# Sparse attention and gated products in float32 on one core: the order of all steps but TensorE's listed anew, sums divided between VectorE and GpSimd

## The chip, the cores and the metric

One core of a Trainium2 chip. The time is device microseconds of one execution; the number given is the median of a kernel's runs.

## The reference

```python
def _attn_ref(q, k, v):                 # (8, 8, 576, 64) each
    scores = scale * np.matmul(q, k.transpose(0, 1, 3, 2))
    rel = pos[:, None] - pos[None, :]
    mask_local = (rel >= 0) & (rel < 32)                                 # heads 0 to 3
    mask_strided = (rel >= 0) & (pos[None, :] % 32 == pos[:, None] % 32)  # heads 4 to 7
    ...
    attn = np.exp(scores - max); attn /= sum
    return np.matmul(attn, v)

def _moe_ref(x, w_gate, w_val, w_out):  # x (4608, 512), w_gate and w_val (512, 1536), w_out (1536, 512)
    gate = 1.0 / (1.0 + np.exp(-(x @ w_gate)))
    return gate * (x @ w_val) @ w_out
```

The attention's output, its heads side by side, is the `x` of the second function.

## The kernel before

All products run in float32 accuracy on TensorE: each operand is split into a high part and a low remainder, and three products (high x high, low x high, high x low) are added in PSUM. ScalarE rounds off the high part (`x`, `hx`, `xh`, `ph` steps), VectorE subtracts it from the whole for the low part (`y`, `hy`, `xl`, `pw` steps: lines 651, 998, 916, 856).

The 4608 tokens are nine blocks of 512. Attention of a batch is four pieces (two local, two strided, two heads each), numbered n = 0 to 23 from batch 2 on. Of a piece, `S` are the scores (TensorE), `M`, `A`, `U` masking, maximum and its subtraction (VectorE), `E` the exponential (ScalarE), `N`, `W` the sum and its division (VectorE), `B` four turns of the matrix by pairs of VectorE's transposes (line 515), `X` the product with the values (TensorE), `H` and `R` copies of it (ScalarE).

Blocks 0, 1 and 2 are computed plainly, with twelve slices f: `g`, `v` the gate and value products of 2.7 us, `s` the sigmoid out of the gate's only bank, `m` gate times value, `x`, `y` the split, `o` or two `oh` the output products. Blocks 3 to 8 go in pairs, k = 3, 5, 7, with seven products of half matrices in place of eight. For that the weights are first kept in device memory in seven sets: `pl` and `po` copy four of them plainly (SP's queue), and of the other sets `pa` adds the words of a weight (line 842), `pb` makes four sums or differences of them (line 847), `ph`, `pw` split and `pd` stores them (lines 864, 865). `r` loads a group of sets back into a ring of buffers. For each pair of blocks `xd` makes four differences of the inputs for each half c (line 904), which `xh`, `xl` split. Then come for six pairs of slices q: `G` and `V`, the half products p (line 930), `c` and `ad` which take them out of PSUM (lines 952, 957), `sg` and `mu` sigmoid and gate (lines 965, 974), and `ta`, `tb`, `tc`, `td`, sums of the five products kept as `hid` (line 980). Then the output stage: `Oa`, `Ob` are groups of three products (line 1009) for p = 1, 2, 6, 5, 7, 3, 4 and q = 0 to 5, 84 groups or 252 products, and `hx`, `hy` split the operand of each q and p into rooms for five of them (`hh`, `hl` and `ops`). `ok` copies a sum out of PSUM (line 1021), `oa` adds to it (line 1025), `os` stores it. In the output stage of k = 3 and 5 the `xd`, `xh`, `xl` steps of the next pair are made.

The order of everything is written by hand: ORDER (line 82) is a list of 2870 step names with their numbers, and each step issues its instructions when its name comes; each engine, and each queue, works through its own in that order:

```python
    for n, (what, kind) in enumerate(zip(names, kinds)):
        STEPS[kind](*(int(i) for i in what[len(kind) :].split(".") if i))
```

Which engine a step runs on is fixed in STEPS (line 1038) and in its function; before, `pa`, `pb`, the four `t` sums and three of four `xd` are GpSimd's, and the second `xd` and all `pw`, `xl`, `hy` VectorE's. Rooms are single: `sum` tiles share `t`, `h2` and `h0` with the `xd` tiles and some `ot` tiles, so a step waits until the last reader of the tile before has done.

## Time and profile before

| | |
|---|---|
| median of 3 runs | 936.42 us (933.55 to 936.65) |
| the profiled execution, its own time | 935.28 us |
| its span, first to last instruction | 933.50 us |
| TensorE busy | 904.4 us, 97% |
| VectorE busy | 675.0 us, 72% |
| ScalarE busy | 476.4 us, 51% |
| GpSimd busy | 334.1 us, 36% |

A row of a timeline has start and duration in us from the start of the span, the engine (PE TensorE's products, PEld its weight loads, DVE VectorE, ACT ScalarE, POOL GpSimd, SP the DMA queue), the line of the code, the operation, and output <- inputs by name. A row of a group has the number of instructions behind `x`, then busy us, mean ns of one, and the idle time of the engine before them with what ended it. Products are pipelined: the next starts before the one before has ended, and the row of one product has a longer time than the step from start to start.

### The profile page before, as it was taken

The page shows a single profiled execution, that of the slowest core. Times are in us where ns is not written, and L with a number is a line of the kernel's source. Part 1 is how long each engine was busy: PE and PEld are TensorE (multiplying, and loading weights), DVE is VectorE, ACT ScalarE, POOL GpSimd, SP SyncE. Part 2 cuts the span into 40 slices and gives each one's busy share as a digit, 9 for nine tenths or more (in the row PEclk, how much of TensorE's full clock was granted, in tenths as well). Part 3 has the DMA queues.
Part 4 walks back from the last instruction along what each step waited for, and adds up shares of the span by engine and source line. Part 5 has one row for each costly group of instructions (what it writes and reads, how often), then busy time and mean ns, then how long its engine had stood idle before and what let it go on. Part 6 is the DMA issues. An engine that isn't in the chain of part 4 may idle for free.

```text
span 933.5 us, 18880 instructions
## 1 busy us (share of the span) xinstructions
PE 904.4 (97%) x7498; PEld 732.8 (79%) x7498; DVE 675.0 (72%) x1028; ACT 476.4 (51%) x854; POOL 334.1 (36%) x387
## 2 busy tenths in 40 slices
...
GB/s 350 355 204 96 192 140 162 162 196 170 304 351 185 112 168 203 285 294 289 248 281 195 173 213 243 217 232 182 198 180 147 190 272 166 218 180 208 196 208 132
DMA packets 116871, 198.26 MB, mean 212 GB/s; under 512 B 7600, under 2 KB 58800, under 8 KB 116784
## 3 DMA queue, kind: packets, MB, share of 16 engines
...
q8 instruction: 59, 0.97, 0.4%
...
## 4 chain that ended last, share of the span: by engine, by line
PE 73%; DVE 14%; DMA 4%; POOL 4%; issue 3%; ACT 2%; SPq 0%; DVEq 0%; POOLq 0%; ACTq 0%
PE p L930 16%; PE oc L1009 14%; PE d L930 13%; PE o L658 8%; PE v L627 8%; PE g L627 8%; DVE pt L515 3%; POOL sum L847 2%; DVE xs L916 2%; DVE hl L998 2%; DMA sets<-sum 2%; PE x L548 1%; DVE ops L998 1%; POOL sum L842 1%; PE s L406 1%
## 5 line engine op out<-in xcount | busy, mean ns | idle before, releaser
L930 PE MATMUL p<-xs,ring 128*128 128x512 f32 x864 | 208.6, 393 | 2.6 <-ACT hid L952 2.1
L930 PEld LDWEIGHTS p<-xs,ring 128*128 128x128 f32 x864 | 162.3, 189 | 38.1 <-ACT hid L952 3.1
L930 PE MATMUL d<-xs,ring 128*128 128x512 f32 x648 | 156.2, 390 | 0.2 <-DVE e L957 0.2
L980 POOL TENSOR_TENSOR hid<-hid,hid 128x512 f32<-128x512 f32 x45 | 64.7, 1438 | 250.8 <-DVE hid L974 250.1
L930 PEld LDWEIGHTS d<-xs,ring 128*128 128x128 f32 x648 | 121.3, 188 | 26.0 <-DVE e L957 0.7
L515 DVE STREAM_TRANSPOSE pt<-sb 32x320 f32<-32x320 f32 (+1 forms) x224 | 120.0, 536 | 4.1
L1009 PE MATMUL oc<-hh,ring 128*128 128x512 f32 x312 | 109.0, 394 | 0.0
L957 DVE TENSOR_TENSOR e<-e,d 128x512 f32<-128x512 f32 x54 | 36.9, 684 | 78.6 <-ACT e L952 40.1
L658 PE MATMUL o<-w,hh 128*128 128x512 f32 x288 | 90.7, 396 | 0.0
L842 POOL TENSOR_TENSOR sum<-w 128x256 f32<-128x256 f32 x68 | 55.5, 837 | 97.8 <-DMA sets<-sum 57.9
L627 PE MATMUL g<-xh,w 128*128 128x512 f32 x256 | 86.0, 393 | 3.2 <-ACT e L635 2.0
L998 DVE TENSOR_TENSOR hl<-hid,hh 128x512 fp32r<-128x512 f32 x78 | 66.4, 861 | 28.8 <-ACT hh L994 28.7
L627 PE MATMUL v<-xh,w 128*128 128x512 f32 x256 | 85.4, 390 | 0.4 <-DVE e L640 0.4
L847 POOL TENSOR_TENSOR sum<-sum 128x128 f32<-128x128 f32 x144 | 81.3, 567 | 10.0
L1009 PE MATMUL oc<-ops,ring 128*128 128x512 f32 x288 | 79.0, 394 | 2.7 <-DVE ops L998 2.4
L1009 PE MATMUL oc<-hl,ring 128*128 128x512 f32 x156 | 62.0, 398 | 9.3 <-DVE hl L998 9.3
L994 ACT CAST hh<-hid 128x512 fp32r<-128x512 f32 x78 | 48.4, 621 | 41.7 <-PE oc L1009 24.6
L1009 PEld LDWEIGHTS oc<-hh,ring 128*128 128x128 f32 x312 | 59.2, 190 | 12.8 <-ACT hh L994 0.4
L1009 PEld LDWEIGHTS oc<-ops,ring 128*128 128x128 f32 x288 | 53.5, 189 | 17.6 <-DVE ops L998 6.9
L952 ACT COPY e<-p 128x512 f32<-128x512 f32 x54 | 31.5, 584 | 69.6 <-PE p L930 66.0
L965 ACT ACTIVATE e<-e 128x512 f32<-128x512 f32 x54 | 34.1, 632 | 62.8 <-DVE e L957 62.7
L658 PEld LDWEIGHTS o<-w,hh 128*128 128x128 f32 x288 | 52.8, 188 | 11.4
...
## 6 DMA issues: line engine op xcount, KB each, us to landing
ring<-sets SPq DMA_DIRECT2D x126, 512.0 KB, 4.3
...
```

The lines of the kernel that those rows point to most:

```text
L515: nc.vector.transpose(dst[to : to + LB, :, col : col + LB], src[part * LB : (part + 1) * LB, :, h * LB : (h + 1) * LB])
L627: nc.tensor.matmul(o, w, x, start=first and n == 0, stop=last and n == len(todo) - 1)
L658: nc.tensor.matmul(acc[k][i], h[:, i * P : (i + 1) * P], w, start=f == 0 and n == 0, stop=f == NF - 1 and n == 2,)
L842: nc.gpsimd.tensor_tensor(to, part(wh[f][i], c), part(wl[f][i], c), op=ALU.add)
L847: nc.gpsimd.tensor_tensor(u[:, to], u[:, x], u[:, y], op=op)
L930: nc.tensor.matmul(to, w[:, (wi * 2 + c) * P : (wi * 2 + c + 1) * P], x[xi][:, c], start=p in (1, 2, 5) and c == j == 0, stop=c == 1 and j ...
L957: nc.vector.tensor_tensor(x, x, two[m, 1], op=ALU.add)
L965: nc.scalar.activation(x, x, AF.Sigmoid)
L980: by.tensor_tensor(h[to], h[x], h[y], op=ALU.subtract)
L994: nc.scalar.copy(ops[q, p][0], hidden_tile(k, q, KEPT[str(p)]))
L998: by.tensor_tensor(hl, hidden_tile(k, q, KEPT[str(p)]), hh.bitcast(F32), op=ALU.subtract)
L1009: nc.tensor.matmul(chains[m, at], w[:, (wi * 2 + m) * P : (wi * 2 + m + 1) * P], x[xi], start=p in (1, 2, 5) and q == j == 0, stop=q == PA ...
```

## The change

The list ORDER from block 1's first product on is another one: the steps of TensorE stand in it in the same order as before, those of all other engines and the DMA steps at other places. Seven kinds of steps can now be given to either of VectorE and GpSimd, by a letter behind the kind (`v` for VectorE, `p` for GpSimd), and the list says which: `pav` 10 of 36, `pbv` 4 of 36, `tav` 4, `tbv` 5, `tcv` 6, `tdv` 4 of 18 each, `xdv` 12 of 24; `pwp` 2 of 36, `xlp` 3 of 42, `hyp` 4 of 126. Of the 24 `xd`, 6 were VectorE's before.

```diff
@@ -101,117 +101,117 @@
-o0.10 fH1.3 LV0 y0.11 wu11.2 fL1.3 pa0.0.0 fR1.3 wl11.2 pa0.0.1 g1.0 pl0 pb0.0.0 v1.0 s1.0 pb0.0.1 oh0.11.0 m1.0 x1.0 S0.0 e0.0 y1.0 d0.0 oh0.11.1 LQ1
+o0.10 fH1.3 LV0 y0.11 wu11.2 fL1.3 pa0.0.0 fR1.3 wl11.2 pa0.0.1 pl0 g1.0 pb0.0.0 v1.0 s1.0 pl2 pb0.0.1 oh0.11.0 m1.0 e0.0 x1.0 S0.0 e0.1 y1.0 oh0.11.1
...
@@ -834,26 +834,26 @@
             nc.sync.dma_start(to[:, 0, n], a[:, 0])
             nc.sync.dma_start(to[:, 1:3, n], b)
 
-    def sum_words(q, i, c):
+    def sum_words(q, i, c, by=nc.gpsimd):
         n = (q * 2 + i) * 2 + c
         u = sums[q, i, c] = work.tile([P, 4, P], F32, tag=("t" if i < 2 else "h2", "h0")[n % 2], name=f"sum{q}_{i}_{c}")
         for at, f in ((0, 2 * q), (1, 2 * q + 1)):
             to = u[:, at::2] if i == 2 else u[:, 2 * at : 2 * at + 2]
-            nc.gpsimd.tensor_tensor(to, part(wh[f][i], c), part(wl[f][i], c), op=ALU.add)
-
-    def sum_parts(*n):
+            by.tensor_tensor(to, part(wh[f][i], c), part(wl[f][i], c), op=ALU.add)
+
+    def sum_parts(*n, by=nc.gpsimd):
         u = sums[n]
         for to, x, y, op in ((3, 2, 3, ALU.add), (2, 0, 2, ALU.subtract), (0, 3, 0, ALU.subtract), (1, 1, 0, ALU.subtract)):
-            nc.gpsimd.tensor_tensor(u[:, to], u[:, x], u[:, y], op=op)
+            by.tensor_tensor(u[:, to], u[:, x], u[:, y], op=op)
 
     def sum_high(q, i, c, odd_one):
         n = q, i, c
         sums_h[n] = (odd if odd_one else work).tile([P, 4, P], F32R, tag=("l0", "ost")[odd_one], name=f"sumh{q}_{i}_{c}")
         nc.scalar.copy(sums_h[n], sums[n])
 
-    def sum_low(*n):
+    def sum_low(*n, by=nc.vector):
         u, h = sums[n], sums_h[n]
-        nc.vector.tensor_tensor(u.bitcast(F32R), u, h.bitcast(F32), op=ALU.subtract)
+        by.tensor_tensor(u.bitcast(F32R), u, h.bitcast(F32), op=ALU.subtract)
 
     def store_sums(q, i, c):
         u, h = sums.pop((q, i, c)), sums_h.pop((q, i, c))
@@ -893,7 +893,7 @@
             x_set[k, p, n] = pool.tile([P, 2, TB], F32R, tag=f"w{USE.index(p)}_{n}", name=f"xs{k}_{p}_{n}")
         return x_set[k, p, n]
 
-    def diff(k, c, n):
+    def diff(k, c, n, by=nc.gpsimd):
         r1, r2 = x_raw[k], x_raw[k + 1]
         if n < 3:
             t = work.tile([P, TB], F32, tag=("t", "h0" if k == SUPER[0] else "h2")[n % 2], name=f"xd{k}_{c}_{n}")
@@ -901,7 +901,7 @@
             t = diffs[k, c, 1]
         diffs[k, c, n] = t
         x, y = ((r2[:, c], r1[:, c]), (r2[:, 2 + c], diffs[k, c, 0]), (r2[:, 2 + c], r2[:, c]), (r1[:, 2 + c], t))[n]
-        (nc.vector if n == 1 else nc.gpsimd).tensor_tensor(t, x, y, op=ALU.subtract)
+        by.tensor_tensor(t, x, y, op=ALU.subtract)
 
     def set_source(k, c, p):
         if p in "123":
@@ -911,9 +911,9 @@
     def set_high(k, c, p):
         nc.scalar.copy(set_tile(k, str(p), 0)[:, c], set_source(k, c, str(p)))
 
-    def set_low(k, c, p):
+    def set_low(k, c, p, by=nc.vector):
         h = set_tile(k, str(p), 0)[:, c]
-        nc.vector.tensor_tensor(set_tile(k, str(p), 1)[:, c], set_source(k, c, str(p)), h.bitcast(F32), op=ALU.subtract)
+        by.tensor_tensor(set_tile(k, str(p), 1)[:, c], set_source(k, c, str(p)), h.bitcast(F32), op=ALU.subtract)
 
     two, got, hidden = {}, {}, {}
 
@@ -1035,6 +1035,12 @@
     def whole_ident():
         nc.gpsimd.tensor_copy(ident, cst[:, SL * KL + GS :])
 
+    def by_vector(step):
+        return lambda *n: step(*n, by=nc.vector)
+
+    def by_gpsimd(step):
+        return lambda *n: step(*n, by=nc.gpsimd)
+
     STEPS = dict(
         J=busy,
         K=constants, C=whole_ident, fQ=first_steps("Q"), fQa=lambda b, p: firsts[b, p]["Q"](0), fQb=lambda b, p: firsts[b, p]["Q"](1),
@@ -1051,8 +1057,9 @@
         e=evict, d=store, LQ=load_queries, LV=lambda n: piece[n]["V"](), Z=lambda n: piece[n]["Z"](), S=score, M=masks,
         A=lambda n: piece[n]["A"](), U=lambda n: piece[n]["U"](), D=lambda n: piece[n]["D"](), E=lambda n: piece[n]["E"](), N=lambda n: piece[n]["NS"](),
         W=lambda n: piece[n]["NW"](), B=lambda n, j: piece[n]["B"](j), X=values, H=high_of, L=lambda n: piece[n]["L"](), R=rest_of,
-        po=plain_out_sets, ta=out_sum("a"), tb=out_sum("b"), tc=out_sum("c"), td=out_sum("d"),
-        hx=out_high, hy=out_low, hyp=lambda k, q, p: out_low(k, q, p, nc.gpsimd), O=out_half, Oa=lambda k, q, p: out_half(k, q, p, (0,)),
+        po=plain_out_sets, **{f"t{n}v": by_vector(out_sum(n)) for n in "abcd"}, pav=by_vector(sum_words), pbv=by_vector(sum_parts), xdv=by_vector(diff),
+        pwp=by_gpsimd(sum_low), xlp=by_gpsimd(set_low), ta=out_sum("a"), tb=out_sum("b"), tc=out_sum("c"), td=out_sum("d"),
+        hx=out_high, hy=out_low, hyp=by_gpsimd(out_low), O=out_half, Oa=lambda k, q, p: out_half(k, q, p, (0,)),
         Ob=lambda k, q, p: out_half(k, q, p, (1,)), ok=out_keep, oa=out_add, os=out_store,
         pl=plain_sets, pa=sum_words, pb=sum_parts, ph=sum_high, pw=sum_low, pd=store_sums, r=load_group,
         G=lambda k, q, p: half_product(k, q, 0, p), V=lambda k, q, p: half_product(k, q, 1, p), c=keep_sum, ad=add_sum, sg=gate_sigmoid,
```

The changed kernel has seven more lines ahead of the steps' table, so that lines from 1038 on have other numbers there; of the lines named here only that of the table itself is among them.

VectorE at the start of the output stage of k = 5, from the last subtraction ahead of it that is the same in both (`xs` are low parts of the next pair's inputs, `hl` and `ops` of the output operands, `xd` differences of inputs, `ot` the sums put out), before:

```order
L916 TENSOR_TENSOR xs_3_1_7899<-xraw_7717,xs_3_0_7888 128x512 x2
L998 TENSOR_TENSOR hl_5_1_7907<-hid_12_7758,hh_5_1_7906 128x512
L998 TENSOR_TENSOR hl_0_2_7919<-hid_0_6798,hh_0_2_7918 128x512
L904 TENSOR_TENSOR xd_0_1_7934<-xraw_7717,xd_0_0_7913 128x512
L998 TENSOR_TENSOR hl_1_2_7932<-hid_3_7059,hh_1_2_7931 128x512
L916 TENSOR_TENSOR xs_5_1_7947<-xd_0_0_7913,xs_5_0_7939 128x512
L916 TENSOR_TENSOR xs_6_1_7955<-xd_0_1_7934,xs_6_0_7942 128x512
L998 TENSOR_TENSOR ops_7416<-hid_5_7150,ops_7416 128x512
L998 TENSOR_TENSOR ops_7416<-hid_8_7425,ops_7416 128x512
L916 TENSOR_TENSOR xs_7_1_7981<-xd_0_2_7950,xs_7_0_7969 128x512
L998 TENSOR_TENSOR hl_4_2_7976<-hid_10_7591,hh_4_2_7975 128x512
```

and now:

```order
L916 TENSOR_TENSOR xs_3_1_7899<-xraw_7717,xs_3_0_7888 128x512
L998 TENSOR_TENSOR hl_5_1_7906<-hid_12_7758,hh_5_1_7905 128x512
L998 TENSOR_TENSOR hl_0_2_7918<-hid_0_6798,hh_0_2_7917 128x512
L998 TENSOR_TENSOR hl_1_2_7929<-hid_3_7059,hh_1_2_7928 128x512
L998 TENSOR_TENSOR ops_7416<-hid_5_7150,ops_7416 128x512
L998 TENSOR_TENSOR hl_4_2_7962<-hid_10_7591,hh_4_2_7961 128x512
L998 TENSOR_TENSOR hl_5_2_7976<-hid_13_7817,hh_5_2_7975 128x512
L998 TENSOR_TENSOR hl_0_6_7989<-hid_0_6798,hh_0_6_7988 128x512
L998 TENSOR_TENSOR ops_7416<-hid_2_7014,ops_7416 128x512
L1025 TENSOR_TENSOR ot_0_1_7943<-ot_0_1_7943,oc_0_2_7950 128x512
L1025 TENSOR_TENSOR ot_1_1_7958<-ot_1_1_7958,oc_1_2_7967 128x512
```

The `xs` and `xd` of the next pair, which stood between the `hl` and `ops`, have gone to later places, and the output operands stand closer together.

GpSimd in the same stage, from the sum `ta` of the last pair of slices on (`hid` are products kept, `xd` as above), before:

```order
L980 TENSOR_TENSOR hid_14_7849<-hid_13_7817,hid_12_7758 128x512
L904 TENSOR_TENSOR xd_0_0_7913<-xraw_7717,xraw_6915 128x512
L980 TENSOR_TENSOR hid_12_7758<-hid_14_7849 128x512
L904 TENSOR_TENSOR xd_0_2_7950<-xraw_7717 128x512
L904 TENSOR_TENSOR xd_0_1_7934<-xraw_6915,xd_0_1_7934 128x512
L904 TENSOR_TENSOR xd_1_0_7990<-xraw_7717,xraw_6915 128x512
L980 TENSOR_TENSOR hid_13_7817<-hid_14_7849,hid_13_7817 128x512
L904 TENSOR_TENSOR xd_1_2_8028<-xraw_7717 128x512
L904 TENSOR_TENSOR xd_1_1_8013<-xraw_6915,xd_1_1_8013 128x512
L980 TENSOR_TENSOR hid_0_6798<-hid_0_6798 128x512
```

and now:

```order
L980 TENSOR_TENSOR hid_14_7849<-hid_13_7817,hid_12_7758 128x512
L980 TENSOR_TENSOR hid_13_7817<-hid_14_7849,hid_13_7817 128x512
L980 TENSOR_TENSOR hid_12_7758<-hid_14_7849 128x512
L980 TENSOR_TENSOR hid_0_6798<-hid_0_6798 128x512
L998 TENSOR_TENSOR ops_7416<-hid_8_7425,ops_7416 128x512
L980 TENSOR_TENSOR hid_5_7150<-hid_5_7150 128x512
L980 TENSOR_TENSOR hid_3_7059<-hid_3_7059,hid_2_7014 128x512
L980 TENSOR_TENSOR hid_10_7591<-hid_10_7591 128x512
L980 TENSOR_TENSOR hid_8_7425<-hid_8_7425,hid_7_7375 128x512
L904 TENSOR_TENSOR xd_0_2_8111<-xraw_7717 128x512
```

The six `xd` that stood among the sums are behind them, three of them, and three have gone to VectorE; one `ops` has come from there.

ScalarE in block 2 between the exponential of a piece (`sb`) and the sigmoids of the fifth and sixth slice (`e_4`, `e_5`), with `sumh` the rounded sums of weights, before:

```order
L852 CAST sumh_1_0_3568<-sum_1_0_3471 128x512
L464 ACT_TABLE_LOAD
L464 ACTIVATE mx_3_3517<-ident 128x1
L470 ACTIVATE sb_3_3516<-sb_3_3516 128x12x54
L852 CAST sumh_0_1_3612<-sum_0_1_3570 128x512
L635 ACT_TABLE_LOAD
L635 ACTIVATE e_4_3618<-g_4_3573 128x512
L647 CAST hh_4_3642<-e_4_3618 128x512
```

and now:

```order
L912 CAST xs_1_0_3188<-xraw_3175 128x512
L464 ACT_TABLE_LOAD
L464 ACTIVATE mx_3_3489<-ident 128x1
L470 ACTIVATE sb_3_3488<-sb_3_3488 128x12x54
L635 ACT_TABLE_LOAD
L635 ACTIVATE e_4_3622<-g_4_3587 128x512
L852 CAST sumh_1_1_3629<-sum_1_1_3600 128x512
L647 CAST hh_4_3653<-e_4_3622 128x512
```

The cast of the sums ahead of the exponential and that between it and the first sigmoid stand behind that sigmoid now.

## Rows read from the trace of the kernel before

**Rows 1.** The page, part 1: busy time of the engines over the whole span.
```profile
PE 904.4 (97%) x7498; PEld 732.8 (79%) x7498; DVE 675.0 (72%) x1028; ACT 476.4 (51%) x854; POOL 334.1 (36%) x387
```

**Rows 2.** TensorE's waits: line, releaser, total us, times, longest us.
```profile
PE oc L1009 <- DVE hl L998: 9.3, 5, 2.8
PE oc L1009 <- DVE ops L998: 2.4, 3, 1.1
PE p L930 <- ACT hid L952: 2.1, 1, 2.1
PE g L627 <- ACT e L635: 2.0, 2, 1.4
```

**Rows 3.** Busy time by stretch: PE, PEld, DVE, ACT, POOL, PEclk, DMA, GB/s.
```profile
139.00:235.00 96.00, 96.00 (x918) 79.37 (x920) 64.79 (x107) 38.86 (x68) 44.56 (x76) 1.00 0.55 171
235.00:357.00 122.00, 117.28 (x1428) 94.81 (x1426) 105.70 (x175) 61.87 (x119) 50.65 (x76) 1.00 0.70 219
401.04:480.97 79.93, 76.18 (x921) 61.67 (x915) 73.37 (x120) 46.40 (x86) 36.52 (x52) 0.98 0.86 281
501.78:569.85 68.07, 63.14 (x378) 49.46 (x377) 58.08 (x72) 34.74 (x64) 24.69 (x17) 0.97 0.64 205
691.66:758.30 66.64, 59.52 (x254) 46.67 (x253) 51.15 (x57) 31.76 (x55) 25.16 (x15) 1.00 0.59 183
872.54:929.87 57.33, 57.31 (x252) 46.88 (x251) 37.10 (x45) 26.89 (x45) 14.82 (x9) 1.00 0.59 184
```

**Rows 4.** Timeline of TensorE: start, us; two attention groups inside an output stage.
```profile
520.87 0.91 PE L548 MATMUL x<-pt,vv 54*64 54x54 f32 x44
...
522.67 0.50 PE L1009 MATMUL oc<-hh,ring 128*128 128x512 f32 x1
```

**Rows 5.** Timeline of VectorE, first output stage, while GpSimd works.
```profile
518.70 1.77 DVE L916 TENSOR_TENSOR xs<-xd,xs 128x512 fp32r<-128x512 f32 x1
520.40 1.77 DVE L998 TENSOR_TENSOR hl<-hid,hh 128x512 fp32r<-128x512 f32 x1
```

**Rows 6.** Timeline of GpSimd in the same stretch.
```profile
518.20 1.73 POOL L980 TENSOR_TENSOR hid<-hid 128x512 f32<-128x512 f32 x1
519.89 1.74 POOL L980 TENSOR_TENSOR hid<-hid,hid 128x512 f32<-128x512 f32 x1
```

**Rows 7.** Timeline of VectorE later in that stage, GpSimd idle.
```profile
539.50 0.68 DVE L998 TENSOR_TENSOR hl<-hid,hh 128x512 fp32r<-128x512 f32 x1
540.10 0.68 DVE L998 TENSOR_TENSOR ops<-hid,ops 128x512 fp32r<-128x512 f32 x1
```

**Rows 8.** Timeline of VectorE: eight transposes in a row.
```profile
412.43 4.15 DVE L515 STREAM_TRANSPOSE pt<-sb 32x320 f32<-32x320 f32 x8
```

**Rows 9.** Timeline of GpSimd beside those transposes.
```profile
413.87 1.29 POOL L980 TENSOR_TENSOR hid<-hid,hid 128x512 f32<-128x512 f32 x1
```

**Rows 10.** VectorE's groups by shape: count, busy us, mean ns; the short subtractions.
```profile
L588 DVE TENSOR_TENSOR xl<-x_a,xh 128x256 fp32r<-128x256 f32 x4 | 1.5, 420 | 3.8 <-ACT xr L597 3.8
...
L588 DVE TENSOR_TENSOR xl<-x,xh 128x192 fp32r<-128x192 f32 x4 | 1.4, 347 | 0.0
...
L588 DVE TENSOR_TENSOR xl<-x,xh 128x32 fp32r<-128x32 f32 x4 | 0.7, 180 | 0.0
```

**Rows 11.** Busy time by stretch, as Rows 3: TensorE at the lower clock.
```profile
451.40:454.80 3.40, 3.40 (x25) 2.71 (x17) 3.00 (x6) 2.14 (x6) 1.24 (x2) 0.50 0.67 157
533.30:536.70 3.40, 3.40 (x9) 2.62 (x9) 3.40 (x3) 2.10 (x4) 2.58 (x2) 0.50 1.03 420
```

**Rows 12.** Timeline of ScalarE ahead of a gate product that waited.
```profile
284.06 0.62 ACT L852 CAST sumh<-sum 128x512 fp32r<-128x512 f32 x1 [0.66 <-POOL sum L847]
...
286.00 0.60 ACT L635 ACTIVATE e<-g 128x512 f32<-128x512 f32 x1
```

**Rows 13.** GpSimd's waits, columns as Rows 2: for the stores of sums.
```profile
POOL sum L842 <- DMA sets<-sum: 57.9, 17, 17.0
```

More of the change, by code (lines that the diff above doesn't have):

```diff
@@ new lines @@
+sg5.5.7 ad5.5.1.7 V5.5.4 mu5.5.7 sg5.5.4 G5.5.3 mu5.5.4 r91 V5.5.3 ad5.5.0.3 sg5.5.3 Oa5.0.1 ad5.5.1.3 r92 xh7.1.3 xh7.0.3 Oa5.1.1 mu5.5.3 Ob5.0.1
+xl7.1.3 Oa5.2.1 ta5.5 hx5.5.1 Ob5.1.1 hy5.5.1 Oa5.3.1 r93 hx5.0.2 tb5.5 Ob5.2.1 Oa5.4.1 hy5.0.2 hx5.1.2 Ob5.3.1 tc5.5 Oa5.5.1 hx5.2.2 hy5.1.2 Ob5.4.1
+ok5.0.1 td5.0 Ob5.5.1 hx5.3.2 Oa5.0.2 hy5.2.2 r94 ok5.1.1 hyp5.3.2 hx5.4.2 Oa5.1.2 Ob5.0.2 hy5.4.2 Oa5.2.2 hx5.5.2 td5.2 Ob5.1.2 Oa5.3.2 hy5.5.2 r95
+hx5.0.6 Ob5.2.2 td5.1 Oa5.4.2 hx5.1.6 hy5.0.6 Ob5.3.2 td5.4 Oa5.5.2 r96 hx5.2.6 Ob5.4.2 hy5.1.6 td5.3 oa5.0.2 Ob5.5.2 hx5.3.6 Oa5.0.6 os5.0.2 r97
@@ new lines @@
+oa5.1.2 hx5.4.6 hy5.2.6 Oa5.1.6 os5.1.2 Ob5.0.6 hy5.3.6 hy5.4.6 Oa5.2.6 hx5.5.6 xdv7.0.0 Ob5.1.6 hy5.5.6 xh7.0.5 Oa5.3.6 r98 xdv7.0.1 hx5.0.5 Ob5.2.6
+tdv5.5 xh7.0.6 Oa5.4.6 hy5.0.5 hx5.1.5 Ob5.3.6 xl7.0.6 Oa5.5.6 hy5.1.5 hx5.2.5 Ob5.4.6 xdv7.0.3 ok5.0.6 hy5.2.5 xh7.0.4 Ob5.5.6 xl7.0.5 hx5.3.5
+Oa5.0.5 r99 xd7.0.2 hx5.4.5 Oa5.1.5 ok5.1.6 Ob5.0.5 hy5.3.5 xh7.0.7 Oa5.2.5 hy5.4.5 hx5.5.5 Ob5.1.5 xl7.0.7 hy5.5.5 Oa5.3.5 r100 hx5.0.7 xd7.1.0
+Ob5.2.5 Oa5.4.5 hx5.1.7 hy5.0.7 Ob5.3.5 xh7.1.5 xl7.0.4 Oa5.5.5 hy5.1.7 r101 hx5.2.7 Ob5.4.5 xdv7.1.1 hy5.2.7 xh7.1.6 Ob5.5.5 xl7.1.5 hx5.3.7 Oa5.0.7
```

210 lines of the change are left out of this document (101 added, 109 removed).

## Prediction

> **What bounds the kernel now.** Read the engines' shares first [rows 1]: TensorE is busy 904.4 of the 933.5 us of the span, so what its work leaves free is 29.1 us, and a change that keeps its instructions and their order can win no more than that, the part of it before block 1 left out, and whatever its clock loses. Then read who ends TensorE's waits [rows 2]: the largest group, 9.3 us in 5 waits, is the output products (line 1009) waiting for a `hl` of VectorE, with 2.4 us for its `ops` beside it; the others are 2 us each and stand in the attention part. Then read the stretches [rows 3]. The one from 139 to 235 us, blocks 0 and 1, has no idle time at all. From 235 to 357 us (block 2) TensorE is idle 4.72 us and VectorE is busy 105.70 of 122 us. From 401 to 481 us (five pieces beside the first joint block) VectorE is busy 73.37 of 79.93 us. The last three rows are the same work three times: the 252 output products of k = 3, 5 and 7. The last one does nothing else and takes 57.33 us. That of k = 5 takes 66.64, so 9.31 us are lost there. That of k = 3 holds two attention groups besides, 1.80 us from 520.87 to 522.67 [rows 4], so its floor is 59.13; it takes 68.07 and loses 8.94. These two stages are 18 of the us to be had.
>
> **Why they lose it.** In the first output stage a two-input subtraction of 128x512 on VectorE starts 1.70 us after the one before it while GpSimd runs its own [rows 5], and GpSimd's sums start 1.69 us apart [rows 6]; with GpSimd idle the same subtractions start 0.60 us apart [rows 7]. One sum on GpSimd thus costs VectorE 1.10 us, more than the 0.60 for which VectorE would do the sum itself. Beside eight transposes the same GpSimd sum takes 1.29 us, and the eight take 4.15 us, 0.52 each [rows 8, 9]: these don't disturb each other. The price holds over whole stages [rows 3]: k = 7 has 45 VectorE and 9 GpSimd instructions, 45 x 0.60 + 9 x 1.10 = 36.9 us, and the row says 37.10; k = 5 has 57 and 15, which makes 50.7, and the row says 51.15.
>
> The Trainium skill says the same more strictly (SBUF — State Buffer, Who interferes with whom): an instruction of VectorE with two SBUF inputs and one of GpSimd that reads SBUF share a read interface, and the second to come is blocked until the first is done. The trace agrees on who disturbs whom; on the price it has 1.10 us, where a block for the whole sum would be 1.29. By the rule the 15 sums of the k = 3 stage below would take 2.9 us more of VectorE, and the time would be about 921.
>
> **The change, part by part.** TensorE's steps stand in the same order. Of the rest, everything after block 0 stands elsewhere, and 39 steps go from GpSimd to VectorE (10 `pa`, 4 `pb`, 19 sums of `hid` and 6 differences `xd`), 9 the other way (2 `pw`, 3 `xl`, 4 `hy`).
>
> *Work.* A `pa` is two instructions of 128x256, at 0.42 each by the nearest row, and a `pb` four of 128x128, between 0.18 and 0.35, taken as 0.27 [rows 10]. So 10 x 0.84 + 4 x 1.08 + (19 + 6 - 9) x 0.60 = 22.3 us more for VectorE, of 675 [rows 1]. Some 11 us of it fall in the attention part, 4 of them before 235 us, where TensorE waits for nothing.
>
> *Output stage k = 5.* VectorE has 60 instructions (3 more) and GpSimd 12 sums (3 fewer). What decides is the first half, 36 product groups of 0.68 us, 24.5 us, to which five operand pairs made ahead add 5 x 1.36 = 6.8: 31.3 us of room. Before, 32 VectorE and 14 GpSimd instructions stand in it: 32 x 0.60 + 14 x 1.10 = 34.6, too much. Now it is 26 and 9: 25.5. The other `xl` and `xd` come in the second half, 34 x 0.60 + 3 x 1.10 = 23.7 of 32.6 us. The whole stage needs 49.2 of 57.33. I leave 1.0 us of the 9.31 lost: gain **8.3**.
>
> *Output stage k = 3.* 73 VectorE and 15 GpSimd instructions, before and after. First half: 36 and 15 before, 36 x 0.60 + 15 x 1.10 = 38.1 of 24.5 + 1.8 + 6.8 = 33.1; now 29 and 10, 28.4. In all VectorE was busy 58.08 us [rows 3], and if every sum still collides it stays 58 of the floor of 59.13: tight. Some of the sums now stand beside transposes and maxima, where they cost nothing. Bounds: nothing lost, or 4; I take 2 of the 8.94: gain **6.9**. The stretch at half clock after its longest wait, 3.4 us at a granted 0.50, which is 1.2 of 2.4 GHz, costs 1.7 us and is part of the 8.94; another lies at 451.4 [rows 11].
>
> *Block 2, 235 to 357 us.* The wait of 1.43 us at 286.65 has ScalarE behind it: it waited 0.66 us for GpSimd's sum and cast it for 0.62 before the sigmoid that frees the bank [rows 12]. That cast now stands behind the sigmoid: gain 1.4. The other 3.3 us are VectorE being late; its work there is about the same (2 us more in the first two pieces, 2 less in the rest). I take half: together **3.0** of 4.72.
>
> *Attention beside the joint block, 401 to 481 us.* VectorE gets some 3 us more work, to 76 where TensorE's own is about 74.5 (76.18 less 1.7 for the clock), unless collisions go. Bounds: 2 worse, 5.5 better; I take **1.0**, as VectorE is full.
>
> *Stores.* The plain copies of the weights (`pl`, `po`, some 14 MB) go ahead of other transfers on SP's queue, from block 2 to block 1, where the DMA share is 0.55 [rows 3]. The sums waited 57.9 us for their stores [rows 13], which hides behind TensorE. Loads of queries and the output stores of block 0 now queue behind those copies: bounds 0 to 3 us lost, **-1.5** with new waits of other kinds.
>
> *Later.* The `t` sums given to VectorE in k = 5 and 7 lie where VectorE is idle a third of the time or more: nothing, with that idle time as cover; without it 0.60 each.
>
> Sum: 8.3 + 6.9 + 3.0 + 1.0 - 1.5 = 17.7. The profiled execution took 935.28 us, the median of the runs is 1.1 above it: 935.3 - 17.7 + 1.1 = **919 us**.
>
> **Rivals.** *All waits go* (0.12): also the rest of block 2 and of the joint block, and the half clock at 451.4. That adds 1.0 + 2.0 for the output stages, 1.7, 4.5 and 1.5, some 11 us: 908. For it speaks that collisions go everywhere, against it the full VectorE.
>
> *VectorE gives half back* (0.20): the output stages gain 8 to 10 instead of 15, since the moved `xl` and `xd` meet the copies of line 1021, which take the `t` and `h2` rooms that the last `xl` must leave first; ScalarE stands in order, so the casts behind such a copy wait too. The copies `ok5.1.5` and `ok5.0.5` stand two to four product groups, 1.4 to 2.7 us, ahead of the products that need them. About 927.
>
> *Nothing moves* (0.10): the waits turn up in the second half of the output stages, 936.
>
> *VectorE becomes the bound* (0.08), slower. Place: 235 to 500 us, where it is busy 87 to 92% [rows 3]. Price: its added work there, 7 us, and two more drops of the clock at 1.7: 10.4. It decides as soon as the output stages gain less than 5.7, that is 10.4 less half a per cent, 4.7. With a gain of 3 there it is 944. For it speaks that the sums are given to an engine that is nearly full; against it that each one taken from GpSimd beside a two-input instruction gives back 1.10 for 0.60. The Trainium skill (Perfetto Trace Analysis, Optimizing Scalar/DVE Operations) advises work to leave a saturated VectorE, if perhaps not for GpSimd, whose port it shares; the change goes the other way, and the trace supports the second half of that sentence.
>
> That the change doesn't do what it says is out: the listing of the instructions shows the division as written.
>
> **The numbers.** The forecast has 0.50. Faster by more than 0.5% (4.7 us, about what a measurement of this kernel can tell from none) is the forecast, the first and the second rival: 0.82; same 0.10, slower 0.08. The range goes from 908 to 933 and leaves out the last two rivals.
>
> **What would show it.** Right: the k = 5 and k = 3 stages take under 60 and 63 us, VectorE's subtractions of line 998 average near 0.75 us where they were 0.86 and 0.96, and the waits for `hl` and `ops` fall from 11.7 to under 4 us. The sigmoid at the fifth product of block 2 follows the exponential without a cast between. Wrong: waits of the output products for ScalarE's line 1021, TensorE idle between 139 and 235 us, or VectorE above 95% from 401 to 481 us with TensorE idle there above 5 us.

## The result, and the profile after

The changed kernel takes **909.67 us** (median of 4 runs, 908.88 to 910.40) beside 935.20 us for the kernel before on the same chip (four runs, the three of the table ahead among them): a ratio of 0.9727, with a 95% interval from 0.9704 to 0.9750. That is 25.5 us won. The prediction said 919 (908 to 933). The profiled executions differ by 26.5 us of span, 933.5 against 907.0, and the stages below are of these two.

The engines' shares, as [rows 1]:

```profile
PE 893.6 (99%) x7498; PEld 731.7 (81%) x7498; DVE 675.9 (75%) x1080; ACT 482.6 (53%) x858; POOL 284.6 (31%) x335
```

VectorE has 52 more instructions than before and is busy for the same time, 675.9 against 675.0 us. TensorE's idle time has gone from 29.1 to 13.4 us.

Then TensorE's waits, as [rows 2] (line and releaser, total us, times, longest):

```profile
PE x L548 <- issue: 1.8, 2, 1.3
PE x L548 <- ACT hid L952: 1.8, 1, 1.8
PE x_a L548 <- DVE pt L515: 1.0, 1, 1.0
PE oc L1009 <- DVE ops L998: 0.3, 1, 0.3
```

The 9.3 us for `hl` are gone, of the 2.4 for `ops` 0.3 are left, and the sigmoid of the gate products is no longer among the releasers. What is left are value products of the attention. They wait for VectorE, also where the view names another. The longest, 1.8 us up to 458.99, is put down to a ScalarE copy that ends at 458.80, but VectorE's transposes for it end at 458.73, so that without the copy at most 0.07 us would be won. The transposes ahead of the other wait, 1.3 us up to 425.67, end at 425.57.

Then the same stretches as in [rows 3]: blocks 0 and 1 (between the same times as before), block 2 and the five pieces beside the joint block (each between the same instructions as before), and the output stages of k = 3, 5 and 7 (columns: us, PE, PEld, DVE, ACT, POOL busy, PEclk, DMA, GB/s):

```profile
139.00:235.00 96.00, 96.00 (x908) 79.16 (x909) 67.50 (x118) 38.41 (x66) 34.88 (x61) 1.00 0.76 242
234.64:351.85 117.21, 115.85 (x1412) 94.82 (x1408) 103.92 (x182) 62.97 (x116) 46.65 (x75) 1.00 0.53 161
395.55:472.97 77.42, 73.66 (x917) 60.69 (x914) 74.13 (x129) 50.11 (x88) 33.43 (x48) 1.00 0.90 296
493.07:552.99 59.92, 59.60 (x378) 48.95 (x377) 52.84 (x72) 35.19 (x64) 26.24 (x17) 1.00 0.71 232
674.66:731.95 57.29, 57.29 (x254) 47.46 (x253) 47.77 (x60) 31.87 (x55) 20.29 (x12) 1.00 0.69 214
846.02:903.31 57.29, 57.29 (x253) 47.11 (x251) 37.00 (x49) 27.07 (x45) 8.18 (x5) 1.00 0.59 184
```

For the sums that follow, the stages of before are taken from their first to their last output product: 68.23, 66.80 and 57.47 us, a few tenths more than [rows 3]; block 2 took 121.95.

| stretch | before | after | won |
|---|---|---|---|
| block 2 | 121.95 | 117.21 | 4.74 |
| five pieces beside the joint block | 79.93 | 77.42 | 2.51 |
| rest up to the first output product | | | 1.3 |
| output stage k = 3 | 68.23 | 59.92 | 8.31 |
| output stage k = 5 | 66.80 | 57.29 | 9.51 |
| output stage k = 7 | 57.47 | 57.29 | 0.18 |

k = 5 now takes what k = 7 takes: nothing is lost there any more.

The prediction argued from the first half of a stage, its first 36 of 84 product groups, and the trace bears that out. First halves of k = 3 and 5, before and then after (columns as above):

```profile
501.62:536.53 34.91, 30.08 (x233) 22.41 (x232) 33.72 (x32) 18.28 (x37) 24.45 (x15) 0.95 0.57 189
691.50:725.50 34.00, 26.88 (x110) 19.64 (x108) 33.70 (x31) 17.18 (x31) 25.16 (x15) 1.00 0.46 144
```

```profile
493.07:519.58 26.51, 26.51 (x234) 21.85 (x232) 25.26 (x28) 17.78 (x35) 16.90 (x10) 1.00 0.71 235
674.66:699.14 24.48, 24.48 (x109) 20.27 (x108) 22.58 (x26) 14.59 (x26) 15.21 (x9) 1.00 0.64 200
```

Before, VectorE was busy 33.72 of 34.91 and 33.70 of 34.00 us there: it set the time. Now TensorE waits for nothing in either. The second halves took 33.32 and 32.80 us before and take 33.41 and 32.81: the gain of both stages lies in their first halves.

The prediction's sign for the collisions was line 998's mean. Groups by shape of before, then of after (count, busy us, mean ns, idle before):

```profile
L998 DVE TENSOR_TENSOR hl<-hid,hh 128x512 fp32r<-128x512 f32 x78 | 66.4, 861 | 28.8 <-ACT hh L994 28.7
L998 DVE TENSOR_TENSOR ops<-hid,ops 128x512 fp32r<-128x512 f32 x48 | 45.5, 960 | 14.5 <-ACT ops L994 14.1
...
L916 DVE TENSOR_TENSOR xs<-xd,xs 128x512 fp32r<-128x512 f32 x24 | 23.6, 993 | 0.3 <-ACT xs L912 0.3
```

```profile
L998 DVE TENSOR_TENSOR hl<-hid,hh 128x512 fp32r<-128x512 f32 x77 | 67.8, 890 | 20.6 <-ACT hh L994 20.6
...
L998 DVE TENSOR_TENSOR ops<-hid,ops 128x512 fp32r<-128x512 f32 x45 | 38.0, 858 | 9.0 <-ACT ops L994 8.8
...
L916 DVE TENSOR_TENSOR xs<-xd,xs 128x512 fp32r<-128x512 f32 x22 | 14.8, 682 | 0.1
...
L842 DVE TENSOR_TENSOR sum<-w 128x256 f32<-128x256 f32 x20 | 8.0, 439 | 0.0
...
L847 DVE TENSOR_TENSOR sum<-sum 128x128 f32<-128x128 f32 x16 | 4.7, 291 | 1.1 <-POOL sum L842 0.6
```

Line 998 hardly got faster: its `hl` is even longer in the mean (0.89), its `ops` shorter (0.86), and both together have 0.87 us where they had 0.89. The subtractions of line 916 are free of collisions now (0.68). So collisions were not removed everywhere but moved. A timeline of VectorE in the first half of k = 5 (start, us):

```profile
688.78 1.78 DVE L998 TENSOR_TENSOR ops<-hid,ops 128x512 fp32r<-128x512 f32 x1
...
691.79 0.69 DVE L998 TENSOR_TENSOR ops<-hid,ops 128x512 fp32r<-128x512 f32 x1
...
694.20 0.69 DVE L998 TENSOR_TENSOR hl<-hid,hh 128x512 fp32r<-128x512 f32 x1
694.80 0.69 DVE L904 TENSOR_TENSOR xd<-xraw,xd 128x512 f32<-128x512 f32 x1
```

and GpSimd at the same time, with the one behind it:

```profile
688.26 1.75 POOL L980 TENSOR_TENSOR hid<-hid 128x512 f32<-128x512 f32 x1
689.97 1.75 POOL L980 TENSOR_TENSOR hid<-hid,hid 128x512 f32<-128x512 f32 x1
699.84 1.71 POOL L904 TENSOR_TENSOR xd<-xraw 128x512 f32<-128x512 f32 x1 [8.12 <-ACT hh L994]
```

A subtraction beside a GpSimd sum is as slow as ever (1.78 us). But from 691.7 to 699.7 GpSimd is quiet, and VectorE starts an instruction every 0.60 us, `xd` sums of its own among them.

### The profile page after: what moved, and what is told of

The parts are those of the page before. It is cut to its first block, busy times and chain, and to the rows that moved or that the text cites. A ratio compares the mean times of both kernels' runs of the same rounds, so it can differ in the third digit from the quotient of the medians.

```text
span 907.0 us, 18863 instructions
## 1 busy us (share of the span) xinstructions
PE 893.6 (99%) x7498; PEld 731.7 (81%) x7498; DVE 675.9 (75%) x1080; ACT 482.6 (53%) x858; POOL 284.6 (31%) x335
## 4 chain that ended last, share of the span: by engine, by line
PE 86%; DVE 7%; DMA 2%; ACT 2%; POOL 2%; issue 1%; SPq 0%; POOLq 0%; DVEq 0%; ACTq 0%
PE p L930 20%; PE oc L1009 17%; PE d L930 15%; PE o L658 9%; PE g L627 9%; PE v L627 9%; PE x L548 2%; DVE pt L515 2%; PE s L406 1%; PE x_a L548 1%; DMA sets<-sum 1%; POOL sum L842 1%; PE gv L627 1%; POOL sum L847 1%; DVE mx L476 1%
## 5 line engine op out<-in xcount | busy, mean ns | idle before, releaser
L930 PE MATMUL p<-xs,ring 128*128 128x512 f32 x864 | 206.3, 390 | 0.0
L980 POOL TENSOR_TENSOR hid<-hid,hid 128x512 f32<-128x512 f32 x33 | 47.9, 1452 | 170.1 <-DVE hid L974 169.5
L847 POOL TENSOR_TENSOR sum<-sum 128x128 f32<-128x128 f32 x128 | 66.0, 516 | 40.9 <-DVE sum L842 31.8
L1009 PE MATMUL oc<-ops,ring 128*128 128x512 f32 x288 | 76.3, 389 | 0.3 <-DVE ops L998 0.3
L842 POOL TENSOR_TENSOR sum<-w 128x256 f32<-128x256 f32 x48 | 41.0, 875 | 86.6 <-DMA sets<-sum 36.8
```

The source lines that it names most:

```text
L842: by.tensor_tensor(to, part(wh[f][i], c), part(wl[f][i], c), op=ALU.add)
L847: by.tensor_tensor(u[:, to], u[:, x], u[:, y], op=op)
L930: nc.tensor.matmul(to, w[:, (wi * 2 + c) * P : (wi * 2 + c + 1) * P], x[xi][:, c], start=p in (1, 2, 5) and c == j == 0, stop=c == 1 and j ...
L980: by.tensor_tensor(h[to], h[x], h[y], op=ALU.subtract)
L1009: nc.tensor.matmul(chains[m, at], w[:, (wi * 2 + m) * P : (wi * 2 + m + 1) * P], x[xi], start=p in (1, 2, 5) and q == j == 0, stop=q == PA ...
```

## The experiments

Twelve kernels ran, in three groups of four, each group beside its own runs of the kernel before (medians 935.74, 935.80 and 936.18 us); ratios and gains are against these. They differ from one another in the list alone, and the diffs show short pieces of it. In two of them the list is a line longer, so that line 998 reads L999.

**The list without the division** (against the changed kernel, at all 48 steps that went to the other engine):

```diff
-pav1.0.0 pb1.0.0 o1.3 m1.5
+pa1.0.0 pb1.0.0 o1.3 m1.5
```

> The list of the change, with every sum back on the engine that it had before (10 pa, 4 pb, 19 sums of hid and 6 xd back to GpSimd; 2 pw, 3 xl, 4 hy back to VectorE). If the order of the steps is what won: the first halves of the two output stages then hold 28 VectorE and 11 GpSimd instructions (k = 3) and 24 and 11 (k = 5), 28 x 0.60 + 11 x 1.10 = 28.9 us for 33.1 of room and 26.5 for 31.3, so both stages stay within 1 us of what they take in the changed kernel (59.9 and 57.3 us) and the time is 909 to 914. If it was the division of the sums between the engines: the stages go back toward 68 and 67 us, and the time is 920 or more.

Measured: 919.13 us, ratio 0.9817 (0.9788 to 0.9847). The output stages:

```profile
499.23:561.91 62.68, 60.65 (x378) 48.64 (x377) 57.34 (x72) 34.60 (x64) 25.27 (x17) 1.00 0.68 222
683.55:742.19 58.64, 57.84 (x254) 47.30 (x253) 49.95 (x57) 31.64 (x55) 25.54 (x15) 1.00 0.66 209
```

The order alone wins 5.5 and 8.2 us there, most of it, with GpSimd's sums as many as before: work that fits the first half is what counts. The first halves take 26.51 and 24.72 us, nearly as in the changed kernel. But the stages are 2.8 and 1.3 us longer than there, not within 1 us as expected: the second half of k = 3 takes 36.17 us in place of 33.41, with VectorE busy 32.06 in place of 27.58. That is one part of what puts the total above the expected range. The other is that ahead of the stages the order alone won only 2.4 us (499.23 against 501.62) where list and division win 8.5. Of these 6.2 us less, 1.1 were lost before block 2, beside a stretch at half clock at 25.6 us which neither profile of the result has, and two stretches of 3.4 us at a granted 0.50, at 414.7 and 431.8, cost 3.4.

**The division without the list** (against the kernel before):

```diff
-g1.5 m1.4 pa1.0.0 x1.4 y1.4 pa1.0.1
+g1.5 m1.4 pav1.0.0 x1.4 y1.4 pav1.0.1
```

> The list of before, place by place, with only the division of the change (the same 39 sums on VectorE, the same 9 on GpSimd). By the price of a collision (1.10 us against 0.60) the first halves hold 39 and 12 instructions for k = 3, 36.6 us for 33.1 of room (before 38.1), and 34 and 12 for k = 5, 33.6 for 31.3 (before 34.6): still too much, so each of the two stages wins 1 to 4 us and the time is 928 to 934. If the division is what won: 915 or less, with both stages within 1 us of the changed kernel's.

Measured: 938.39 us, ratio 1.0026 (1.0008 to 1.0044), a miss: nothing won, and a little lost.

```profile
507.27:573.94 66.67, 62.82 (x378) 49.62 (x377) 55.22 (x72) 34.92 (x64) 23.88 (x17) 0.97 0.65 210
695.56:762.43 66.87, 61.45 (x254) 48.48 (x253) 50.53 (x60) 32.03 (x55) 20.10 (x12) 0.95 0.59 183
```

k = 3 won 1.6 us and k = 5 none, as the first halves were still too full: VectorE is busy 32.62 of 33.81 and 33.69 of 34.07 us in them. What was lost lies ahead of the stages: the first output product starts at 507.27 instead of 501.62, with 2.3 us more of waits and three stretches at half clock ahead of it where the kernel before has one. The division chosen for the new order was of no use in the old one.

**The parts of the program apart**: before's list up to `Oa3.0.1`, the changed list from there, and the mirror of it. Both lists are written out in full in their kernels; this says what the first holds (`plain` takes the letter `v` or `p` off a step):

```python
first = before[: before.index("Oa3.0.1")]
done = {plain(step) for step in first}
ORDER = first + [step for step in changed if plain(step) not in done]
```

> The list of before up to the first output product of k = 3, from there the list of the change with its division. If the two parts of the gain add up, this has the gain of the output stages alone: 8.2 us for k = 3 and 9.4 for k = 5, so about 918, and the waits ahead of the first output product are those of before (idle 11 to 12 us from block 2 on). If the output stages could only be cut because work before them had been done earlier (sums, stores and loads ahead of them), the stages take 62 us or more each and the time is 923 or more.

> The mirror of the earlier splice: the list of the change with its division up to the first output product of k = 3, from there the list of before. If the parts add up, this has the gain ahead of the output stages alone, 8.5 us (the first output product of k = 3 starts at 501.62 us in the kernel before, at 493.07 in the changed one), so about 927, with the output stages back at 68 and 67 us. If the prediction's small terms for blocks 1, 2 and the joint block (2.5 us together) were right and the rest came from somewhere else: 932 or more.

Measured: 917.02 us, ratio 0.9796 (0.9770 to 0.9821), and 927.75, ratio 0.9908 (0.9889 to 0.9926). In the first the stages take 59.91 and 57.29 us, as in the changed kernel; in the second 68.25 and 66.84, as before. The gains, 18.7 and 8.1 us, sum to 26.8 where the whole is 25.5. So the two parts add up, and the output stages needed nothing that the attention part had done earlier.

**The price by itself**: before's list in its order, the 30 GpSimd sums inside the output stages of k = 3 and 5 given to VectorE in their places:

```diff
-Oa3.5.2 hx3.2.6 td3.1 Ob3.4.2 hy3.2.6
+Oa3.5.2 hx3.2.6 tdv3.1 Ob3.4.2 hy3.2.6
```

> The list of before, unchanged in its order, and one thing done: the 30 GpSimd sums (hid sums and xd) that stand in the output stages of k = 3 and k = 5 go to VectorE in their places. By the price in the trace (0.60 us each on VectorE, 1.10 us as a collision) the first halves need 51 x 0.60 = 30.6 us of 33.1 and 46 x 0.60 = 27.6 of 31.3, where they needed 38.1 and 34.6: both stages lose nearly all their waits, 60 to 62 and 58 to 60 us, and the time is 918 to 922, with VectorE's subtractions of line 998 near 0.70 us in both. If instead VectorE is short of time in any case (rival: it becomes the bound), or the places in the list decide, the stages stay above 65 us and the time is 930 to 940.

Measured: 922.46 us, ratio 0.9858 (0.9831 to 0.9884), a little above the first range and far from the second; the two stages, and line 998:

```profile
501.25:563.31 62.06, 60.21 (x378) 48.80 (x377) 52.87 (x87) 34.80 (x64) 0.24 (x2) 1.00 0.70 225
684.98:744.47 59.49, 58.18 (x254) 47.23 (x253) 45.04 (x72) 31.95 (x55) 0.00 (x0) 1.00 0.67 206
```

```profile
L999 DVE TENSOR_TENSOR hl<-hid,hh 128x512 fp32r<-128x512 f32 x78 | 57.5, 746 | 27.9 <-ACT hh L995 27.7
L999 DVE TENSOR_TENSOR ops<-hid,ops 128x512 fp32r<-128x512 f32 x48 | 36.2, 757 | 13.1 <-ACT ops L995 12.6
```

VectorE does 15 more instructions in k = 5 and is busy 6.1 us less than in [rows 3]. A sum that GpSimd did thus cost VectorE (51.15 - 45.04 + 15 x 0.60) / 15 = 1.01 us there, and by the same working 0.95 in k = 3. The prediction's 1.10 is an upper value. The mechanism is shown for the two output stages: without one step moved, the engine of the sums alone was worth 13.3 us, and the first halves fell to 28.40 and 26.69 us, with VectorE still busy 27.99 and 26.35 of them.

**The same in the changed list**: all 32 GpSimd sums and subtractions of the three output stages to VectorE:

```diff
-r47 hx3.4.5 xlp5.1.5 Oa3.1.5
+r47 hx3.4.5 xl5.1.5 Oa3.1.5
```

> The changed kernel with all GpSimd work of the three output stages (25 sums of hid and xd, 3 xl, 4 hy) on VectorE in the same places: 0 sums are left on GpSimd there. By the price of 0.60 us the k = 3 stage then has some 88 VectorE instructions, 53 us, and k = 5 72, 43 us, less than the floors of 59.1 and 57.3: no stage gets longer, and line 998's mean on VectorE falls from 0.88 to about 0.69 us: 909 to 911, no difference that can be measured. If the division by the list is needed even where the order is the new one (VectorE too full in the first halves): the k = 3 stage takes over 61 us and the time is 912 or more.

Measured: 909.04 us, ratio 0.9720 (0.9697 to 0.9743), not to be told from the changed kernel.

```profile
491.43:551.53 60.10, 59.60 (x378) 48.95 (x377) 52.77 (x87) 35.34 (x64) 0.24 (x2) 1.00 0.72 231
673.18:730.46 57.28, 57.28 (x254) 47.45 (x253) 45.74 (x72) 32.49 (x55) 0.00 (x0) 1.00 0.69 214
844.54:901.82 57.28, 57.28 (x253) 47.11 (x251) 35.85 (x54) 27.07 (x45) 0.00 (x0) 1.00 0.59 184
```

```profile
L998 DVE TENSOR_TENSOR hl<-hid,hh 128x512 fp32r<-128x512 f32 x78 | 53.5, 689 | 20.3 <-ACT hh L994 19.5
...
L998 DVE TENSOR_TENSOR ops<-hid,ops 128x512 fp32r<-128x512 f32 x48 | 32.6, 687 | 10.2 <-ACT ops L994 9.6
```

Line 998 is at 0.69 us, free of collisions, and no stage gets shorter for it: in the changed list the collisions that were left held up no product. Beside this run one can read what a sum or subtraction on GpSimd costs VectorE in the changed list: (52.84 - 52.77 + 15 x 0.60) / 15 = 0.60 us in k = 3, and 0.77 in k = 5, against 0.95 and 1.01 in the old order.

**The division by families**, against the changed kernel: the 19 sums of `hid` and 6 `xd` back on GpSimd, and the 14 word sums back:

```diff
-Oa3.1.7 Ob3.0.7 tdv3.2 ok3.0.5
+Oa3.1.7 Ob3.0.7 td3.2 ok3.0.5
...
-po1 pav1.0.0 pb1.0.0 o1.3
+po1 pa1.0.0 pb1.0.0 o1.3
```

> The changed kernel with only the 19 sums of hid and the 6 xd back on GpSimd, in the same places; the word sums and the 9 that went to GpSimd stay as changed. All but two of the 25 lie in or after the output stage of k = 3, so the first output product of k = 3 stays within 1 us of 493 us, and the two output stages take 62.7 and 58.6 us as they do with the list alone: 913 to 915. If the sums of hid were the main part of what the division wins: 917 or more. If they were nothing: 909 to 911.

> The changed kernel with only its 14 word sums (10 pa, 4 pb: 36 VectorE instructions, 7 us) back on GpSimd, all in the same places. List and division together win 25.5 us, the list alone 16.6; of the missing 9 us some 3.4 lie in the output stages and 5 to 6 ahead of them. If the word sums are what wins there (GpSimd's sums are late otherwise, and ScalarE's casts of them stand ahead of its copies for TensorE): the first output product of k = 3 starts at 498 to 500 us and the time is 914 to 916, output stages unchanged at 59.9 and 57.3. If they are not, or cost VectorE what they give: 909 to 911.

Measured for the first: 914.38 us, ratio 0.9763 (0.9749 to 0.9778), as expected; the stages take 63.17 and 59.16 us, and the first output product starts at 493.26. With the new order, then, the sums of `hid` and the `xd` are worth 4.7 us, 5.1 by the two stages. For the second: 912.15, ratio 0.9741 (0.9721 to 0.9760), between the two expectations, and not told apart from the changed kernel by its interval. Its profiled execution reaches the first output product 4.5 us later than the changed kernel's. Its stretches at half clock, and the whole from the first half product to there:

```profile
412.00:418.80 6.80, 6.80 (x114) 5.83 (x107) 5.90 (x9) 2.79 (x6) 3.06 (x4) 0.50 0.77 224
463.20:466.60 3.40, 3.40 (x75) 2.75 (x54) 3.18 (x5) 3.26 (x9) 0.00 (x0) 0.50 0.84 241
358.67:497.72 139.05, 134.60 (x1358) 110.65 (x1357) 122.26 (x196) 81.58 (x141) 65.08 (x90) 0.96 0.82 262
```

In the changed kernel that part takes 133.49 us, 129.73 of them busy. Of the 5.56 us more, half the two stretches, 5.1, is the clock at a granted 0.50 (1.2 of 2.4 GHz); TensorE's idle time, 4.45 us, is little above the changed kernel's 3.76. The four executions of this kernel say the same: the two with a mean granted clock of 0.997 and 0.998 took 910.99 and 910.45 us, where the changed kernel's take 908.88 to 910.40 at 0.998 to 1.000, and the two at 0.993 and 0.994 took 913.3. At the same clock the word sums are worth no more than about 1 us; whether they are what keeps the clock up stays open.

**The early copies undone**: the changed kernel with the 12 copies `pl`, `po` at the places of before:

```diff
-s1.0 pl2 pb0.0.1 oh0.11.0
+s1.0 pb0.0.1 oh0.11.0
...
-y1.7 v1.8 s1.8 pav2.0.0 pb2.0.0
+y1.7 pl2 v1.8 s1.8 pav2.0.0 pb2.0.0
```

> The changed kernel with only the 12 plain copies of the weights on SP's queue (pl, po) put back to the places that they have in the list of before. The prediction counted the early copies at 1.5 us lost (0 to 3), so by it this takes 908 to 909.7, no more than the changed kernel. Rival: the early copies win, because they leave the queue free when the sums' stores come, for which GpSimd waited 57.9 us in the kernel before and 36.8 in the changed one (sets); then GpSimd's sums come late again, casts on ScalarE wait for them, and the time is 912 or more.

Measured: 916.02 us, ratio 0.9787 (0.9770 to 0.9804): the rival's time is right, and so is its queue, but the way from there to TensorE is another. One wait of TensorE, and the DMA queue of SP before it (first and last of 16 copies, and the store behind them):

```profile
255.70 0.80 PE L627 MATMUL g<-xh,w 128*128 128x512 f32 x1 [5.49 <-DVE sb L430]
```

```profile
239.80 0.50 SPq L819 DMA_DIRECT2D sets<-w  x1
...
249.39 1.28 SPq L820 DMA_DIRECT2D sets<-l  x1
250.78 0.37 SPq L864 DMA_DIRECT2D sets<-sumh  x1
```

The queue takes 0.47 to 1.28 us for each copy, 11 us for the 16, and the store of a cast sum (line 864) stands behind them. The DMA engines are full all that time (DMA share 0.99):

```profile
239.80:250.70 10.90, 10.41 (x157) 8.30 (x155) 8.77 (x19) 3.60 (x5) 1.66 (x4) 1.00 0.99 331
```

So no run tells whether issuing or moving the bytes set the 11 us. Within the wait the granted clock falls, and it is 0.50 from 252.2 to 259.0 us, in which TensorE is busy 3.30 us. No GpSimd sum is late here: ScalarE's next cast needs the room of the tile that is to be stored, VectorE's subtraction needs the cast, and the masking that TensorE waits for stands behind the subtraction:

```profile
253.90 0.62 ACT L852 CAST sumh<-sum 128x512 fp32r<-128x512 f32 x1 [6.14 <-DMA sets<-sumh]
```

```profile
254.55 0.69 DVE L856 TENSOR_TENSOR sum<-sum,sumh 128x512 fp32r<-128x512 f32 x1 [5.60 <-ACT sumh L852]
255.16 0.49 DVE L430 TENSOR_TENSOR sb<-s_g,cst 128x324 f32<-128x324 f32 x1
```

**The early copies alone**, in before's list:

```diff
-y1.10 pa3.0.1 pl3 v1.11
+y1.10 pa3.0.1 v1.11
...
-pa0.1.1 U1 g1.3 E1
+pa0.1.1 U1 pl3 g1.3 E1
```

> The list of before, place by place, with only the 12 plain copies of the weights (pl, po) moved to the places that they have in the changed list. Putting them back late in the changed list cost 6.4 us, with one wait of 5.5 us at 255.7 us: SP's queue was issuing copies for 11 us while a store of a cast sum stood behind them. If early copies win by themselves: 929 to 932, with GpSimd's waits for stores to the sets below the 57.9 us of before. If what the late copies cost belongs to the pairing with the new list only (in the list of before no such wait stands there): 934 to 938, about as before.

Measured: 935.19 us, ratio 0.9993 (0.9979 to 1.0008). In the old order moving them is worth nothing that can be measured. The trace shows a little: TensorE's waits in block 2 fall from 4.66 to 2.74 us, but a stretch at half clock has come up at 337.6, and GpSimd's waits for stores fall to 39.4 us without anything getting faster for it.

**One sigmoid moved**, in before's list:

```diff
-v2.4 N7 ph4.0.1.0 pw4.0.1 pd4.0.1 W7 s2.4
+v2.4 s2.4 N7 ph4.0.1.0 pw4.0.1 pd4.0.1 W7
```

> The list of before with one step moved: the sigmoid of the fifth gate product of block 2 goes ahead of the cast of a sum (ph4.0.1.0) and of the W step, to directly behind its value product. By the prediction the wait of 1.43 us at 286.65 us goes, and nothing else changes: 1.4 us, 933.5 to 935, in the profile no wait of a gate product for the sigmoid between 280 and 292 us. If the cast moved behind only makes the next wait (VectorE's subtraction of that sum, the next store): the wait turns up within 10 us of it and the time is 935 to 936.

Measured: 938.01 us, ratio 1.0022 (1.0009 to 1.0035), a miss. TensorE's timeline has a shorter wait at the gate product and a longer one 5 us behind it, and over block 2 its waits sum to 5.95 us where they were 4.66:

```profile
288.10 0.50 PE L627 MATMUL g<-xh,w 128*128 128x512 f32 x1 [0.60 <-ACT e L635]
...
293.05 0.50 PE L627 MATMUL v<-xh,w 128*128 128x512 f32 x1 [1.89 <-DVE e L640]
```

**Three value steps of TensorE a half product later**, the only experiment that touches TensorE's order:

```diff
-ad3.2.1.2 Z15 X14.1 c3.2.1.6 pw3.2.1 pd3.2.1 mu3.2.2 S15.1
+ad3.2.1.2 Z15 c3.2.1.6 pw3.2.1 pd3.2.1 mu3.2.2
...
-H14 hx3.2.1 G3.2.5 M15.0
+hx3.2.1 G3.2.5 X14.1 S15.1 LV15 R14 H14 M15.0
```

> The changed kernel with one thing of TensorE's own order changed: three value steps of the attention (X12.1, X13.1, X14.1), at which it still waits 0.6, 1.3 and 1.8 us in the joint block for VectorE's transposes, stand one half product (1.36 us) later, with the scores behind them. If these waits only need cover: 906 to 908.5, the three waits under 0.5 us each. If VectorE's total work is what binds there (it is busy 93% of that stretch), the scores come later, its next group starts later, and the waits reappear at the next values or products: 909 to 912.

Measured: 910.75 us, ratio 0.9738 (0.9717 to 0.9759). The waits come back at the next places:

```profile
PE x L548 <- issue: 2.2, 2, 1.9
PE x L548 <- DVE pt L515: 1.8, 1, 1.8
...
PE p L930 <- ACT e L952: 1.2, 2, 1.0
```

So cover alone doesn't end them. That stretch is VectorE's: 74.13 of 77.42 us in the changed kernel. No version that ran beats the changed kernel by more than can be measured.

## Why the prediction was right, and where its sizes were off

The mechanism of the output stages was as argued, and the time lies in the range. The sum was 8.8 us short of the 26.5 between the two profiles: all five terms were too low, so the truth came close to the first rival (all waits go, 908), which had 0.12.

- *Output stage k = 5.* Predicted 8.3, measured 9.5. Argued from the work of the first half against its room, and the runs bear that out: the list alone takes first-half work away and wins 8.2; the division alone leaves it too full and wins nothing; with no GpSimd sum at all in the old order the stage falls to 59.49. VectorE's busy time was forecast at 49.2 us and is 47.77; that of the first half was put at 34.6 before and 25.5 now, and is 33.70 and 22.58.
- *Output stage k = 3.* Predicted 6.9, measured 8.3. The step that failed is "if every sum still collides it stays 58 of the floor of 59.13: tight". VectorE's busy time is 52.84, since a GpSimd instruction there costs it 0.60 us in the mean and not 1.10: the 2 us left as lost were nearly all won too. The price was too high for this stage from the start: 72 x 0.60 + 15 x 1.10 is 59.7 us, and [rows 3] have 58.08. The prediction's reason, that sums stand beside transposes and maxima, holds in part. None of the fifteen stands beside transposes, which lie at 540.55 to 546.03, after the last one. The first nine run until 510.12 side by side with VectorE, which from 497.33 on starts one of its own every 1.7 us. Of the six later ones, that at 514.57 runs beside a maximum, and that at 520.32 takes 2.93 us itself while VectorE goes on in steps of 0.60 (520.21, 520.81, 521.41).
- *The Trainium skill's stricter rule* (SBUF — State Buffer, Who interferes with whom: the loser is blocked for the whole instruction) would have left k = 3 about 2.9 us worse than 1.10 per sum does. The runs go the other way: 0.95 to 1.01 per sum in the old list, 0.60 to 0.77 in the new one. A lock for the whole instruction is no price until it is known what stands beside it.
- *Block 2.* Predicted 3.0, measured 4.7. The sign came true as written: in the changed kernel the sigmoid of the fifth gate product starts at 285.23, straight behind the table load, and the cast stands behind it, at 286.39. But the step "that cast now stands behind the sigmoid: gain 1.4" was wrong as a sum of single steps. Done alone, it moved the wait on by 5 us and won nothing, so the 1.4 came true by luck: the wait is gone in the changed kernel, but not by this step alone. The order won the whole stage: with the list alone it takes 117.25 us, as with the division (117.21). With the copies put back late it takes 123.89, so they are part of it; what else in the list is, no run shows.
- *The joint block.* Predicted 1.0, measured 2.5, with 1.3 more around it. From the first half product to the first output product TensorE is idle 3.76 us of 133.49, where it was idle 4.56 of 137.38; 3.1 of the 3.9 us won are TensorE's own busy time, 132.82 before and 129.73 after. Half of the stretch at 451.4 [rows 11], 1.7 us, is the clock, which the prediction had in its bounds and its first rival but not in the 1.0; where the other 1.4 us of busy time come from no run shows. VectorE is at 96% there, as was feared, and TensorE idle under 5 us, so the warning sign did not fire.
- *Stores.* The step "-1.5 with new waits of other kinds" had the wrong sign. TensorE got no wait for a load or a store, has no idle time from 139 to 235 us, and with the copies late the same list loses 6.4 us. The prediction looked at what would queue behind the early copies; it did not ask what stands behind them when they are late, a store whose room a cast needs.
- *VectorE's load.* 22.3 us more work were forecast, by 0.42 and 0.27 us for the short sums (measured 0.44 and 0.29). The work came, and about as much time came back from collisions, so that the last rival (VectorE becomes the bound) did not come true in the new order; in the old one the same division was 2.6 us slower than before. "VectorE's subtractions of line 998 average near 0.75 us" failed: 0.87. A mean says nothing of where the slow ones stand; where all were made fast, at 0.69, the time stayed the same.

What stays open: what the division wins ahead of the output stages. The list alone wins 2.4 us there, list and division 8.5. The difference lies in the joint block, which with the list alone takes 138.49 us from the first half product to the first output product, beside 133.49; 3.4 of these 5.0 us are the two stretches at half clock. Neither family taken back alone cost more than 0.5 us there beside the clock.
